# Strassen's seven products for the second product of eight row tiles in four half layers

## The chip, the cores and the metric

One NeuronCore of a Trainium2 chip runs the program; the time is the device time of one execution in microseconds, the median of several. Times inside an execution come from a hardware profile of one execution, counted from its first instruction. In the profile PE is TensorE (PEld its weight loads), DVE VectorE, ACT ScalarE, POOL GpSimd and SP SyncE.

## The reference

```python
attn = softmax(causal(q @ k.T / 8 + min(bias(s), 0)))       # 2 batches, 8 heads, 576 rows, head size 64
x = rows_of(attn @ v)                                        # 1152 x 512
P = exp(x @ w_gate); 8 x (normalise rows, then columns)      # 1152 x 8
y = sum_e P[:, e:e+1] * (relu(x @ w1[e]) @ w2[e])            # 8 experts, 512 -> 1024 -> 512
out = softplus(y @ w_in) @ w_out                             # 512 -> 2048 -> 512
```

All of it is in 32-bit floats. The change concerns the products `relu(...) @ w2[e]` and `softplus(...) @ w_out`.

## The kernel before

The two feed-forward parts are cut into 20 half layers x, each with 512 hidden columns: 0 to 15 are the halves of the eight experts (NX = 16, gated from XE = 2 on), 16 to 19 the quarters of the last layer (NH = 20). In a half layer the first product makes the hidden columns (`hh`, `hl`, four blocks of 128 by 1152 rows) and the second product multiplies them with 512 x 512 weights and adds into `acc`, nine tiles of 128 rows by 512 columns.

Every number is a high part, rounded for the fast matmul format, and a low part, the rest. ScalarE writes the high part (an activation), VectorE or GpSimd the low part (original minus high). A product of two such numbers is three matmuls: high x high, high x low, low x high. Each matmul loads its own 128 x 128 weights.

The first product already goes by Strassen's algorithm (class `Unit`): seven products of 288 columns, 6 matmuls each, for each of two column halves a and b and each of the two groups g of 576 rows; p1 to p7 name them, so "a6" in a sequence is product 6 of half a. The copies v and u (L275) keep partial sums, the adds at L288, L306 and L317 finish them, and `evict` applies relu or softplus and writes the two parts.

The second product (`downs`) is plain: for a row tile, 4 blocks of hidden columns x 3 matmuls of 512 columns into one PSUM bank (tags y1 and y2 in turn), then one VectorE add of 512 columns into `acc` (`total`, L374 or, with the gate, L377). One step "d" of a sequence is the three matmuls of one block. In the last half layer the last row tile goes in two column halves (`last_rows`, L356) so that its output can leave early.

The order of everything is written out by hand. `play` walks a string: a product or a step "d" for TensorE, and markers that put generators into lists (`back`: "=n" prepares the next first-product weights, "wn" the next second-product weights; `side`: others). After each TensorE item, `step` takes one piece from each list, so the engines' queues receive the side work between the products. Every engine works its queue in order. A_SEQ runs the first product of group 1 of half layer x beside the row tiles 0 to 3; B_SEQ the first product of group 0 of x + 1 beside the row tiles 4 to 8. Here stretch A and stretch B stand for one pass through such a sequence. `defer` and `flush` move an eviction behind the following product.

VectorE also converts the last layer's weights from 64-bit floats in half layers 2 to 12 (`convert`; the pieces go out at L947).

Of the kernel before, what the change touches and what calls it, by code (L numbers as in the profile page):

```python
# [20 lines left out]
def attention_moe_ffn(ctx, tc, q, k, v, s, w_gate, w1, w2, w_in, w_out, out):  # L21
# [105 lines left out]
    w2_p = []  # L127

# [60 lines left out]
    def prep2(x, ft):  # L189
# [5 lines left out]
        hi = w2_p[0].tile([P, DM], F32R, tag=f"w2h{ft}", name=f"w2h{ft}", bufs=1)  # L195
        lo = w2_p[0].tile([P, DM], F32R, tag=f"w2l{ft}", name=f"w2l{ft}", bufs=1)
        wt[x, 2, ft] = (hi, lo)
# [3 lines left out]
        if r:  # L201
            load(x + 1, 2, i)
        yield


    gate_t = []
# [21 lines left out]
    def evict(x, k, z, q, cols):  # L228

        hh, hl = hb[0][:, q, cols], hb[1][:, q, cols]  # L230

# [19 lines left out]
    class Unit:  # L251
# [68 lines left out]
    def downs(x, groups):  # L320

        for tiles in groups:
            py = {}
            for t in tiles:
                nd[0] += 1
# [5 lines left out]
            if x == NH - 1 and tiles[-1] == NTT - 1:  # L331
                nd[0] += 1
                yield from last_rows(x, tiles[0], (py[tiles[0]], ps.tile([P, DM], F32, tag=f"y{1 + nd[0] % 2}", name="py", bufs=1)))
                return
            for k, ft in enumerate((0, 2, 1, 3)):
                wh, wl = wt[x, 2, ft]
# [9 lines left out]

    def last_rows(x, t, banks):

        tsl = slice(t * P, (t + 1) * P)
        for py, cols in zip(banks, (slice(0, DM // 2), slice(DM // 2, DM))):  # L350
            py = py[:, :DM // 2]
            for k, ft in enumerate((0, 2, 1, 3)):
                wh, wl = wt[x, 2, ft]
                hh, hl = hb[0][:, ft, tsl], hb[1][:, ft, tsl]
                for n, (u, v) in enumerate(((hh, wh), (hh, wl), (hl, wh))):
                    nc.tensor.matmul(py, u, v[:, cols], start=(k == 0 and n == 0), stop=(k == NF - 1 and n == 2))  # L356
                flush()
                if k == 1:
                    yield
            a = acc[0][:, t, cols]  # L360
            nc.vector.tensor_tensor(out=a, in0=py, in1=a, op=ALU.add)
            nc.sync.dma_start(out=out[tsl, cols], in_=a)
            yield
# [20 lines left out]
    with tc.manual_schedule():  # L384
# [442 lines left out]
        m_t.append(m_p)  # L827
# [340 lines left out]
```

## Time and profile before

| what | value |
|---|---|
| median of the runs shown (lowest 1075.39, highest 1720.8) | 1075.45 us |
| the profiled execution | 1075.35 us |
| its span, first to last instruction | 1073.6 us |
| TensorE busy | 1058.5 us |
| VectorE, ScalarE, GpSimd busy | 728.7, 504.6, 339.8 us |
| granted TensorE clock, mean | 1.000 |

Busy time of TensorE counts pipelined matmuls, whose ends are modelled; how far one matmul is from the next is read from starts.

### The profile page before, as it was taken

How to read it: one execution, taken by the hardware profiler on the slowest of the kernel's cores; microseconds unless marked ns; L12 is line 12 of the kernel's file. 1: busy time of each engine (PE TensorE's matmuls, PEld its weight loads, DVE VectorE, ACT ScalarE, POOL GpSimd, SP SyncE). 2: the span in 40 equal slices, each digit the busy share in tenths (PEclk: the TensorE clock that was granted, in tenths of full speed). 3: DMA queues.
4: the chain of work that ended last, by engine and by line, in shares of the span. 5: the costliest groups of instructions: out<-in, count | busy, mean ns of one | idle time of the engine just before them, and what ended most of it. 6: DMA issues, size and time to landing. Idle time of an engine off the chain costs nothing.

```text
span 1073.6 us, 17639 instructions
## 1 busy us (share of the span) xinstructions
PE 1058.5 (99%) x6600; PEld 932.5 (87%) x6600; DVE 728.7 (68%) x1626; ACT 504.6 (47%) x1200; POOL 339.8 (32%) x405
## 2 busy tenths in 40 slices
PE   7999999999999999999999999999999999999998
PEld 4777889889898888889888888989888888889887
DVE  6576566767878779687887888784555578545533
ACT  7998544343443434434434433433343367445442
POOL 8885303053332414142342414233030314022100
PEclk9999999999999999999999999999999999999999
DMA  6221111122232321223132222312111101112002
GB/s 197 85 78 55 40 41 40 40 79 99 99 110 83 113 99 70 98 98 122 66 118 99 78 90 98 101 50 87 40 40 40 40 25 56 40 40 79 1 12 77
DMA packets 30525, 78.41 MB, mean 73 GB/s; under 512 B 5744, under 2 KB 11120, under 8 KB 30440
## 3 DMA queue, kind: packets, MB, share of 16 engines
q1 hardware_dynamic: 27696, 68.69, 19.0%
q0 software_dynamic: 2560, 8.39, 2.0%
q8 instruction: 52, 0.85, 0.3%
q14 instruction: 33, 0.27, 0.1%
q10 hardware_dynamic: 184, 0.20, 0.1%
HBM read 65.99 MB, written 10.75 MB: 71 GB/s over the span
## 4 chain that ended last, share of the span: by engine, by line
PE 92%; DVE 3%; ACT 2%; POOL 1%; issue 1%; DMA 1%; SPq 0%; POOLq 0%; ACTq 0%; DVEq 0%
PE py L341 46%; PE ph L267 40%; PE sc L575 1%; PE pv L682 1%; DVE xl L978 1%; PE tr L656 1%; ACT eb L625 1%; DVE xt L1009 1%; POOL eb L638 1%; PE sc L579 0%; PE tr L650 0%; PE pv L692 0%; PE pg L862 0%; ACT pt L670 0%; PE tr L662 0%
## 5 line engine op out<-in xcount | busy, mean ns | idle before, releaser
L267 PE MATMUL ph<-xh,w1h 128*128 128x288 f32 x1120 | 331.7, 296 | 0.3 <-ACT v L275 0.3
L267 PE MATMUL ph<-xh,w1l 128*128 128x288 f32 x1120 | 331.2, 296 | 0.0
L267 PE MATMUL ph<-xl,w1h 128*128 128x288 f32 x1120 | 329.3, 294 | 0.0
L341 PE MATMUL py<-w2h,hh 128*128 128x512 f32 x716 | 284.2, 397 | 1.0 <-DVE acc L371 1.0
L341 PE MATMUL py<-w2l,hh 128*128 128x512 f32 x716 | 283.2, 395 | 0.2 <-POOL w2l L200 0.2
L341 PE MATMUL py<-w2h,hl 128*128 128x512 f32 x716 | 283.1, 395 | 0.0
L267 PEld LDWEIGHTS ph<-xh,w1h 128*128 128x128 f32 x1120 | 210.0, 188 | 21.8 <-ACT v L275 0.5
L267 PEld LDWEIGHTS ph<-xl,w1h 128*128 128x128 f32 x1120 | 210.4, 188 | 20.4
L267 PEld LDWEIGHTS ph<-xh,w1l 128*128 128x128 f32 x1120 | 210.3, 188 | 0.0
L200 POOL TENSOR_TENSOR w2l<-raw,w2h 128x512 fp32r<-128x512 f32 x40 | 55.6, 1389 | 347.1 <-ACT w2h L198 347.0
L275 ACT ACTIVATE v<-ph 128x288 f32<-128x288 f32 x160 | 63.5, 409 | 212.3 <-PE ph L267 209.5
L341 PEld LDWEIGHTS py<-w2h,hl 128*128 128x128 f32 x716 | 134.6, 188 | 32.2
L234 ACT ACTIVATE hh<-ph 128x288 fp32r<-128x288 f32 x192 | 78.5, 411 | 159.6 <-DVE ph L317 80.8
L341 PEld LDWEIGHTS py<-w2h,hh 128*128 128x128 f32 x716 | 134.5, 188 | 12.7 <-DVE acc L371 1.2
L341 PEld LDWEIGHTS py<-w2l,hh 128*128 128x128 f32 x716 | 134.6, 188 | 12.3 <-POOL w2l L200 0.7
L377 DVE SCALAR_TENSOR_TENSOR acc<-py,gate,acc 128x512 f32<-128x512 f32 x126 | 93.9, 745 | 56.8 <-PE py L341 56.7
L152 DVE TENSOR_TENSOR w1l<-raw,w1h 128x512 fp32r<-128x512 f32 (+1 forms) x160 | 105.7, 661 | 15.5 <-ACT w1h L149 15.5
L946 POOL TENSOR_TENSOR cm<-cm,ct 128x512 f32<-128x512 f32 x32 | 45.0, 1408 | 202.5 <-DVE ct L944 202.5
L241 DVE SCALAR_TENSOR_TENSOR hl<-ph,hh 128x288 fp32r<-128x288 f32 x192 | 86.4, 452 | 31.2 <-ACT hh L234 29.5
L149 ACT ACTIVATE w1h<-raw 128x512 fp32r<-128x512 f32 (+1 forms) x160 | 91.3, 570 | 0.0
L306 DVE TENSOR_TENSOR t<-ph,v 128x288 f32<-128x288 f32 x80 | 36.3, 454 | 74.1 <-ACT v L275 73.5
L198 ACT ACTIVATE w2h<-raw 128x512 fp32r<-128x512 f32 x80 | 50.5, 632 | 13.6 <-PE py L341 12.8
(196 smaller groups left out, 1251.0 us busy)
## 6 DMA issues: line engine op xcount, KB each, us to landing
raw<-in_w SPq DMA_DIRECT2D x64, 512.0 KB
f<-in_w_in SPq DMA_DIRECT2D x16, 512.0 KB
f<-in_w_out SPq DMA_DIRECT2D x16, 512.0 KB
wd<-cm POOLq DMA_DIRECT2D x32, 256.0 KB, 3.1
raw<-wd SPq DMA_DIRECT2D x16, 512.0 KB
vv<-in_v SPq DMA_DIRECT2D x8, 256.0 KB
out<-acc SPq DMA_DIRECT2D x8, 256.0 KB
qk<-in_k SPq DMA_DIRECT2D x7, 288.0 KB
```

Source lines behind the costliest of these rows:

```text
L149: nc.scalar.activation(out=hi[:, o], in_=t[:, src], func=AF.Copy)
L152: nc.vector.tensor_tensor(out=lo[:, o], in0=t[:, src], in1=f(hi[:, o]), op=ALU.subtract)
L198: nc.scalar.activation(out=hi, in_=t[:, r], func=AF.Copy)
L200: (nc.gpsimd if i else nc.vector).tensor_tensor(out=lo, in0=t[:, r], in1=f(hi), op=ALU.subtract)
L234: nc.scalar.activation(out=hh, in_=z, func=AF.Relu)
L241: nc.vector.scalar_tensor_tensor(out=hl, in0=z, scalar=0.0, in1=f(hh), op0=ALU.max, op1=ALU.subtract)
L267: nc.tensor.matmul(o, u, v, start=(start and c == 0 and n == 0), stop=(c == 1 and n == 2), skip_group_check=True)
L275: nc.scalar.activation(out=t, in_=self.a, func=AF.Copy)
L306: defer(0, lambda: nc.vector.tensor_tensor(out=t, in0=self.c, in1=u4, op=ALU.add))
L341: nc.tensor.matmul(py[t], u, v, start=(k == 0 and n == 0), stop=(k == NF - 1 and n == 2))
L377: nc.vector.scalar_tensor_tensor(out=a, in0=py, scalar=gate_t[0][:, t, e:e + 1], in1=a, op0=ALU.mult, op1=ALU.add)
L946: nc.gpsimd.tensor_tensor(out=m, in0=m, in1=f(t), op=ALU.add)
```

## The change

In half layers 14, 17, 18 and 19 (`SEVEN`) the second product of row tiles 0 to 3 (g = 0) and 5 to 8 (g = 1) is done by the seven-product algorithm on pairs of row tiles. Four row tiles are two pairs, r = 0 and 1; a pair's 256 rows by 512 hidden columns are the blocks a11, a12, a21, a22, and the 512 x 512 weights the blocks b11 to b22 of 256 x 256. Tile 4, which has 64 rows of each group, stays plain ("m").

- `evict` writes only one 32-bit word per hidden number in these half layers (`word`, into `hw`); the two parts are made later, for whole blocks.
- `h_steps` forms the sums s1 to s4 of the a blocks on GpSimd and splits what is multiplied: "e" does s3 and a11, "E" s2, s1, a22, a12, the rows m and most splits, "F" s4. Each `yield` ends a piece.
- `prep_b` ("x11" and so on) splits a block of the next weights, `prep_t` ("y0" to "y4") forms and splits the sums t1 to t4.
- `pairs` runs the seven products: each is 6 matmuls of 256 columns for each of the two pairs, r = 0 in one PSUM bank and r = 1 in the other, with two halves of a bank for different sums; after each of the 14 steps a VectorE add of 256 columns goes to `acc` (`add_to`), 14 in place of 4 adds of 512.
- New sequences place these pieces; in the last half layer the plain tile is put between the first and the second of the seven products, and `last_rows` goes.
- The second product's weights become two tiles `w2h` and `w2l`, split by ScalarE and VectorE alone where the next half layer is also one of the four and the present one too; a descriptor scratch of 1024 bytes is asked for (the default is larger); the pool `sp` for the new tiles opens in half layers 13 and 16, for which the conversion's pool closes one half layer earlier and the pool `tq` is closed after half layer 16's first stretch.

```diff
+    SEVEN = (NX - 2, NX + 1, NX + 2, NX + 3)
...
+    def prep_b(x, n):
+
+        if x >= NH:
+            return
+        raw = blocks(x)[n]
+        hi, lo = (w2_block(n, z) for z in w2_t)
+        nc.scalar.activation(out=hi, in_=raw, func=AF.Copy)
+        yield
+        nc.vector.tensor_tensor(out=lo, in0=raw, in1=f(hi), op=ALU.subtract)
+        if n == "21":
+            load(x + 1, 2, 1)
+        ready.add((x, "b" + n))
...
+    def prep_t(x, n, kept=True):
+
+        if x >= NH:
+            return
+        b = blocks(x)
+        w = sp_t["x"]
+
+        def sum_(o, a, z, op=ALU.subtract):
+            nc.gpsimd.tensor_tensor(out=o, in0=a, in1=z, op=op)
+
+        if n == 0:
+            sum_(b["11"], b["12"], b["11"])
+            yield
+            sum_(b["12"], b["22"], b["12"])
...
+        elif n == 2:
+            src = w
+            if kept:
+                hold((x, "t"), (None,))
+                sum_(w, b["22"], b["11"])
+            else:
+                sum_(w, w, b["11"], ALU.add)
+            yield
+            yield
+        elif n == 4:
+            src = w
+            sum_(w, b["21"], w)
...
+        t_part(x, n, src, "h")
+        yield
+        t_part(x, n, src, "l")
...
+    def h_steps(x, g, part):
+
+        z = h_sets(g)
+
+        def high(n):
+            nc.scalar.activation(out=z[n][0], in_=z[n][2], func=AF.Copy)
+
+        def low(n):
+            nc.vector.tensor_tensor(out=z[n][1], in0=z[n][2], in1=f(z[n][0]), op=ALU.subtract)
+            ready.add((x, g, n))
+
+        def sum_(o, a, b, op):
+            nc.gpsimd.tensor_tensor(out=z[o][2], in0=z[a][2], in1=z[b][2], op=op)
+
+        if part == "e":
+            hold((x, g), (None,))
+            sum_("s3", "a11", "a21", ALU.subtract)
+            high("a11")
+            yield
+            low("a11")
+            yield
+            last = (x - 1 + g, 1 - g)
+            assert not seven(last[0]) or (*last, "done") in ready
+            high("s3")
+            yield
+        elif part == "E":
+            high("m")
+            high("a22")
+            yield
+            low("s3")
+            low("m")
+            low("a22")
+            sum_("s2", "a22", "s3", ALU.subtract)
+            yield
+            sum_("s1", "a21", "a22", ALU.add)
+            yield
+            high("a12")
+            yield
+            low("a12")
+            high("s2")
+            yield
+            sum_("s4", "a12", "s2", ALU.subtract)
+            high("s1")
+            yield
+            low("s2")
+            low("s1")
+            hold(None, ((x, g),))
+            yield
+        else:
+            high("s4")
+            yield
+            low("s4")
+            yield
+
+    def add_to(x, t, cols, py, first, tile_col):
+        a = acc[0][:, t, cols]
+        if first and x in (0, NX):
+            nc.vector.tensor_copy(a, py)
+        elif x < XE or x >= NX:
+            nc.vector.tensor_tensor(out=a, in0=py, in1=a, op=ALU.add)
+        else:
+            e = x // XE
+            nc.vector.scalar_tensor_tensor(out=a, in0=py, scalar=gate_t[0][:, t, e:e + 1], in1=a,
+                                           op0=ALU.mult, op1=ALU.add)
+        if x == NH - 1 and (not first or (tile_col == (0, 1))):
+            nc.sync.dma_start(out=out[t * P:(t + 1) * P, cols], in_=a)
...
+    def pairs(x, g, middle=None):
+
+        z = h_sets(g)
+        py = []
+        for r in range(2):
+            nd[0] += 1
+            py.append(ps.tile([P, DM], F32, tag=f"y{1 + nd[0] % 2}", name="py", bufs=1))
+        d = (slice(0, HW), slice(HW, 2 * HW))
...
+        for a, b, bank, start, tile_, col, first in (
+                ("a11", "b11", 0, True, 0, 0, True), ("s3", "t3", 1, False, 1, 1, True),
+                ("s2", "t2", 0, False, 1, 0, True), ("a22", "t4", 1, False, 1, 0, False),
+                ("s1", "t1", 0, False, 1, 1, False), ("s4", "b22", 0, False, 0, 1, True),
+                ("a12", "b21", 1, True, 0, 0, False)):
+            if a == "s3" and middle is not None:
+                yield from middle
+            for r in range(2):
+                assert (x, g, a) in ready and ((x, b) in ready or {(x, "w", 2 * (b[1] == "2") + c) for c in range(2)} <= ready), (x, g, a, b)
+                o = py[r][:, d[bank]]
+                for c in range(2):
+                    ops = [(left(0, a, c, r), right(0, b, c)), (left(0, a, c, r), right(1, b, c)),
+                           (left(1, a, c, r), right(0, b, c))]
+                    for n, (u, v) in enumerate(ops):
+                        nc.tensor.matmul(o, u, v, start=(start and c == 0 and n == 0), stop=(c == 1 and n == 2),
+                                         skip_group_check=True)
+                flush()
+                if a == "s4" and r:
+                    ready.add((x, g, "done"))
+                add_to(x, rows_of(g) // P + 2 * r + tile_, d[col], o, first, (tile_, col))
+                yield
...
+        def word():
+            c = slice(cols.start % S, cols.start % S + HB)
+            nc.scalar.activation(out=sp_t["hw"][:, q, c], in_=z, func=AF.Relu if x < NX else AF.Softplus)
+
+        if seven(x):
+            if k < 0:
+                word()
+            else:
+                defer(k, word)
+            return
...
-            evict(self.x, 0, b, self.p, self.h0)
+            evict(self.x, 5 if seven(self.x) else 0, b, self.p, self.h0)
...
-            for k, ft in enumerate((0, 2, 1, 3)):
+            for k, ft in enumerate((0, 1, 2, 3) if seven(x - 1) else (0, 2, 1, 3)):
+                wh, wl = (z[:, ft] for z in w2_t)
...
+        A7_SEQ = "E0 a1 b1 a2 b2 =0 d d a6 d b6 d d F0 a7 d d b7 =1 d d a5 d b5 d d a3 d b3 e1 a4 d b4"
+        A7_LAST = "E0 a1 b1 a2 b2 d a6 d d b6 d d F0 a7 d d b7 d d a5 d b5 d a3 d b3 e1 a4 b4 d d"
+        B7_SEQ = ("E1 a1 b1 =2 a2 b2 d d d d a6 d d {11} b6 d d {3} F1 a7 d b7 d {2} a5 d b5 d {4} d a3 d {1} d b3 e0 d {22} a4 d b4 d {21}")
+        TO_SEVEN = B_SEQ.replace("b2", "b2 y3 y2 y4 y1").replace("b3", "b3 e0")
+        B7 = {True: {"11": "x11 x12 y0", "3": "y3", "2": "y2", "4": "y4", "1": "y1", "22": "x22", "21": "x21"},
+              False: {"11": "w0 w1", "3": "", "2": "", "4": "", "1": "", "22": "", "21": "w2 w3"}}
...
+            if seven(x):
+                if x + 1 < NH:
+                    seq = B7_SEQ
+                    for k, z in B7[seven(x + 1)].items():
+                        seq = seq.replace("{" + k + "}", z)
+                    play(seq, products(x + 1, 0), then(downs(x, [(NB,)]), pairs(x, 1)))
+                else:
+                    play("E1 n n n n " + "d " * 8 + "F1 " + "d " * 10, {}, pairs(x, 1, downs(x, [(NB,)], "tr")))
+                if not seven(x + 1):
+                    rest()
+                    own.close()
+                continue
...
-    nc = bacc.Bacc("TRN2", target_bir_lowering=False, num_devices=1)
+    nc = bacc.Bacc("TRN2", target_bir_lowering=False, num_devices=1, dynamic_dma_scratch_size=1024)
```

(`h_sets`, `rows_of`, `blocks`, `w2_block`, `t_part` and `hold` name parts of tiles, split a T or check the order; `step` takes from a third list `bot`, which holds the "x" and "y" work.)

## Rows read from the trace of the kernel before

**Rows 1.** The page's head, and busy time of each engine over the whole span.

```profile
span 1073.6 us, 17639 instructions
...
PE 1058.5 (99%) x6600; PEld 932.5 (87%) x6600; DVE 728.7 (68%) x1626; ACT 504.6 (47%) x1200; POOL 339.8 (32%) x405
```

**Rows 2.** The chain that ended last: start, us, engine, tile, line, count.

```profile
1033.02 3.99 PE ph L267 x30
...
1054.76 12.60 PE py L341 x54
1067.36 2.81 PE py L356 x24
```

**Rows 3.** Windows: a converting half layer, two late ones, the end.

```profile
core 0: us, PE busy (x) PEld busy (x) DVE busy (x) ACT busy (x) POOL busy (x), PEclk, DMA share, GB/s
334.91:382.39 47.48, 47.48 (x277) 42.56 (x277) 38.48 (x73) 19.35 (x44) 15.57 (x17) 1.00 0.27 95
959.80:1007.28 47.48, 47.48 (x278) 42.56 (x277) 23.50 (x47) 23.46 (x57) 8.42 (x10) 1.00 0.13 45
1007.28:1054.76 47.48, 47.48 (x278) 42.57 (x277) 21.27 (x44) 21.74 (x53) 2.59 (x2) 1.00 0.05 17
1054.76:1073.60 18.84, 15.40 (x79) 12.72 (x77) 5.41 (x10) 0.81 (x2) 0.00 (x0) 0.98 0.23 84
```

**Rows 4.** TensorE's waits: who waited for whom, us in total, times, longest.

```profile
PE sc L575 <- DMA eb<-in_q: 5.5, 1, 5.5
...
PE py L341 <- DVE acc L371: 1.0, 1, 1.0
```

**Rows 5.** Groups by line and form: busy us, mean ns, idle before it.

```profile
L267 PEld LDWEIGHTS ph<-xh,w1h 128*128 128x128 f32 x1120 | 210.0, 188 | 21.8 <-ACT v L275 0.5 <-ACT u L275 0.2
...
L152 DVE TENSOR_TENSOR w1l<-raw,w1h 128x512 fp32r<-128x512 f32 x120 | 89.0, 742 | 15.5 <-ACT w1h L149 15.5
...
L234 ACT ACTIVATE hh<-ph 128x288 fp32r<-128x288 f32 x192 | 78.5, 411 | 159.6 <-DVE ph L317 80.8 <-DVE ph L288 46.0 <-PE ph L267 31.7
L149 ACT ACTIVATE w1h<-raw 128x512 fp32r<-128x512 f32 x120 | 74.9, 624 | 0.0
L275 ACT ACTIVATE v<-ph 128x288 f32<-128x288 f32 x160 | 63.5, 409 | 212.3 <-PE ph L267 209.5
...
L198 ACT ACTIVATE w2h<-raw 128x512 fp32r<-128x512 f32 x80 | 50.5, 632 | 13.6 <-PE py L341 12.8 <-DVE xl L88 0.3
...
L317 DVE TENSOR_TENSOR ph<-ph,u 128x288 f32<-128x288 f32 x80 | 36.7, 458 | 18.9 <-PE ph L267 18.4
...
L947 POOL DMA_DIRECT2D wd<-cm x32 | 19.0, 594 | 9.5 <-POOL cm L946 9.5
```

**Rows 6.** Timeline of VectorE: start, us, instruction, idle before it.

```profile
964.83 0.69 DVE L374 TENSOR_TENSOR acc<-py,acc 128x512 f32<-128x512 f32 x1 [1.95 <-PE py L341]
965.44 0.42 DVE L152 TENSOR_TENSOR w1l<-raw,w1h 128x256 fp32r<-128x256 f32 x1
```

**Rows 7.** Timeline of VectorE in a converting half layer.

```profile
273.17 0.68 DVE L152 TENSOR_TENSOR w1l<-raw,w1h 128x512 fp32r<-128x512 f32 x1
273.77 1.52 DVE L928 TENSOR_SCALAR f<-f 128x512 f32<-128x512 f32 x1
```

**Rows 8.** Timeline of all engines at the end.

```profile
1069.88 0.28 PE L356 MATMUL py<-w2h,hl 128*128 128x256 f32 x1
1070.20 0.42 DVE L361 TENSOR_TENSOR acc<-py,acc 128x256 f32<-128x256 f32 x1 [0.98 <-PE py L356]
```

**Rows 9.** Timeline of GpSimd with VectorE out of its way.

```profile
785.42 1.30 POOL L200 TENSOR_TENSOR w2l<-raw,w2h 128x512 fp32r<-128x512 f32 x1 [30.65 <-ACT w2h L198]
...
789.98 0.73 POOL L158 TENSOR_TENSOR raw<-raw 128x256 f32<-128x256 f32 x1
```

**Rows 10.** Timeline of GpSimd beside rows 7.

```profile
273.33 1.68 POOL L946 TENSOR_TENSOR cm<-cm,ct 128x512 f32<-128x512 f32 x1 [1.69 <-DVE ct L944]
```

**Rows 11.** The line that sends out converted weights, its first and last start.

```profile
L947 POOL DMA_DIRECT2D wd<-cm x32: 557/557/761, 242.7 to 726.4; - x32
```

More of the change, by code (lines that the diff above doesn't have):

```diff
@@ L201, in prep2, with seven, blocks, w2_block @@
         if r:
+            assert not seven(x) or (x, "raw") in ready
             load(x + 1, 2, i)
+        ready.add((x, "w", ft))
         yield
+    def seven(x):
+        return x in SEVEN
+    def blocks(x):
+        r1, r2 = raw_t[x, 2, 0], raw_t[x, 2, 1]
+        return {"11": r1[:, :, :HW], "12": r1[:, :, HW:], "21": r2[:, :, :HW], "22": r2[:, :, HW:]}
+    def w2_block(n, z):
+        f0 = 2 * (n[0] == "2")
+        c0 = HW * (n[1] == "2")
+        return z[:, f0:f0 + 2, c0:c0 + HW]
@@ new lines, in prep_b, with hold @@
+    def prep_b(x, n):
[10 more added lines that the diff above has]
+        yield
+    held = [None]
+    def hold(who, after):
+        assert held[0] in after, (held, who)
+        held[0] = who
@@ L206, in attention_moe_ffn @@
+    ready = set()
     gate_t = []
@@ L318, in p4, with downs @@
             evict(self.x, 0, self.c, self.p + 2, self.h0)
-    def downs(x, groups):
+    def downs(x, groups, bank=None):
         for tiles in groups:
@@ L324, in downs @@
             for t in tiles:
+                if bank:
+                    py[t] = ps.tile([P, DM], F32, tag=bank, name="pyt", bufs=2)
+                    continue
                 nd[0] += 1
@@ L330, in downs @@
                     nc.gpsimd.tensor_scalar(a, a, gate_t[0][:, t, 0:1], 1.0, ALU.mult, ALU.mult)
[L331 to L334, printed above, removed]
-            for k, ft in enumerate((0, 2, 1, 3)):
-                wh, wl = wt[x, 2, ft]
+            if seven(x):
+                assert {(x, g, "m") for g in range(B)} <= ready
+            for k, ft in enumerate((0, 1, 2, 3) if seven(x - 1) else (0, 2, 1, 3)):
+                wh, wl = (z[:, ft] for z in w2_t)
+                assert (x, "w", ft) in ready or {(x, f"b{1 + ft // 2}{c}") for c in (1, 2)} <= ready, (x, ft)
                 for t in tiles:
@@ L345, in downs @@
                     yield
[L347 to L363, printed above, removed]
     def total(x, t, py):
@@ L827, in attention_moe_ffn @@
         m_t.append(m_p)
+        w2_t.extend(w2_p[0].tile([P, NF, DM], F32R, name=n) for n in ("w2h", "w2l"))
         hb.append(m_p.tile([P, NF, NT], F32R, name="hh"))
@@ L1023, in attention_moe_ffn, with open_blocks @@
         side = []
+        bot = []
+        def open_blocks():
+            stack = ExitStack()
+            sp = stack.enter_context(tc.tile_pool(name="sp", bufs=1, reuse_waits="tile"))
+            for n in ("h", "l"):
+                sp_t["s" + n] = sp.tile([P, 2, 2, 2, P], F32R, name="s" + n)
+                sp_t["t" + n] = sp.tile([P, 4, 2, HW], F32R, name="t" + n)
+            sp_t["hw"] = sp.tile([P, NF, S], F32, name="hw")
+            sp_t["x"] = sp.tile([P, 2, HW], F32, name="xw")
+            return stack
         tick = [0, 0, 0, 0]
@@ L1039, in step @@
                 next(conv, None)
-            for todo in (back, side):
+            for todo in (back, side, bot):
                 while todo and next(todo[0], 1):
@@ L1044, in rest @@
         def rest():
-            for todo in (back, side):
+            for todo in (back, side, bot):
                 for z in todo:
```

102 lines of the change are left out of this document (92 added, 10 removed).

## The prediction

> **What bounds the kernel now.** I read the page's head first: TensorE is busy for 99% of the span [rows 1]. That alone proves little, since matmuls are pipelined. So next the chain that ended last, in order of time [rows 2]: from the first half layer on it is TensorE alone, 30 matmuls of 288 columns in 3.99 us (133 ns each), 54 of 512 in 12.60 (233 ns), 24 of 256 in 2.81 (117 ns). Columns set the pace: 0.456 to 0.462 ns per column in all three, with no fixed part that grows when a matmul is shortened. A half layer is 168 x 133 + 108 x 233 ns = 47.5 us, and the windows show 47.48 with TensorE busy for all of it [rows 3]. Its list of waits has no line from these stages over 1.0 us [rows 4]. So a column removed is time saved, and anything that makes TensorE wait is time lost, one for one. VectorE is busy for 23.5 of 47.48 us, ScalarE 23.5, GpSimd 8.4 [rows 3]. The clock is 1.00 throughout; it drops nowhere in these stages.
>
> **What is saved.** Four row tiles cost 4 x 4 x 3 = 48 matmuls of 512 columns, 48 x 233.3 ns = 11.20 us. By Strassen they cost 7 x 2 x 2 x 3 = 84 of 256, 84 x 117 = 9.83 us. The 117 ns includes a weight load before every matmul, as it does here. Saved: 1.37 us a group; eight groups (two in each of four half layers) 10.97 us. The last tile's two column halves become one plain tile: 2.81 against 2.80, nothing. So the floor is 1075.35 (the profiled run, 1.75 over its span; the median is 0.1 higher) - 10.97 = 1064.4. This is 1.0%, while about 2% is what a measurement of this kernel can tell from no change: at its very best the change stays inside that bound.
> [...]
>
> **What the side engines get.** Durations are from [rows 5]; back to back, VectorE starts the next instruction some 0.08 us before the listed end (0.69 takes 0.61, 0.68 takes 0.60) [rows 6, 7], so I use 0.60 for a 512-element split, 0.38 for a 288-column add, 0.34 for a 256-element split. The 256-column add lasts 0.42 [rows 8]: 0.35 back to back. In stretch A (14 first products at 0.80 us, 14 Strassen steps at 0.70: 21.0 us): 14 adds 4.9, 7 splits of 512 4.2, the 64-row split 0.34, 6 adds of the first product 2.3, 4 weight splits 2.4: 14.1 us, 67%. In stretch B between two Strassen half layers (23.8 us): 4.9 + 0.6 for the plain tile + 15 splits 9.0 + 0.34 + 2.3 + weights 1.9 = 19.0 us, 80%. The converting half layers have VectorE at 38.48 of 47.48 us, 81%, with TensorE never idle [rows 3], so the amount alone is no stall. ScalarE goes to some 31 of 44.8 us (16 first evictions at 0.41, 22 splits at 0.63 and 2 shorter, weights and copies 9.5). GpSimd has 8 sums of 0.73 as now, plus 12 of twice the size, 1.30 (a split of that size took as much, undisturbed) [rows 9]: 21.4 us. None is full.
>
> **What the trace says about the order of it.** [...] A GpSimd sum that began at 273.33 took 1.68 us where 1.30 is its like undisturbed: the difference is what was left of a VectorE split begun at 273.17, which gave way at 273.77 [rows 7, 9, 10]. The VectorE instruction that followed at 273.77 then lasted 1.52 us, past the sum's end at 275.01. The kernel has 10 GpSimd instructions in such a half layer now [rows 3]; with the change it has 20, twelve of them long, tied to VectorE's splits in a chain. So I walk the queues at the start of a stretch, where the chain stands.
>
> *Stretch A.* TensorE's nominal times: a1 to 0.8, b1 1.6, a2 2.4, b2 3.2, a11 on both banks 4.6, a6 5.4, s3 first bank 6.1, b6 6.9, s3 second 7.6, and s2 would start at 7.6. On VectorE s3, m and a22 are split by 3.2 (ScalarE passes a22 at 2.5), which lets GpSimd form s2 (3.2 to 4.5). VectorE splits a12 (4.5 to 5.1), GpSimd forms s1 (5.1 to 6.4), VectorE's split of s2 stands behind that (6.4 to 7.0), GpSimd's first weight sum slips in (0.75), and the split of s1 ends at 8.4. Only then, in the queue's order, comes the add of s3's first bank: it releases the bank at 8.85, and s2 stalls 1.25 us. If GpSimd wins each contest it is 2.1. If s2 need not wait for the add of the bank's other half, it is 0. The trace of before has no matmul into one half of a bank while the other half is being read, so that is open; every hand-over in it goes by the whole bank, so I take the wait as there. Its size I halve, to 0.6: the walk starts VectorE with a full queue and charges it for each contest, while the converting half layers have the same contests (two within 3 us in [rows 7, 10]), VectorE at 81%, and not one wait of TensorE. Four times: 2.4 (0 to 8.4).
> [...]
>
> *Stretch B.* The same chain starts with E1, but VectorE's queue puts the plain tile's total behind the split of s1, at 8.1 to 8.5, ending at 8.7 to 9.1. The bank of the plain tile is the second one of the new pair, wanted at 7.5: a stall of 1.3 to 1.7 by the same walk, 0 if GpSimd's sums fall between the splits. Halved for the same reason, 0.65. Three such stretches: 2.0 (0 to 5.1).
> *The two B's with new blocks* (half layer 17 to 18, 18 to 19) add four GpSimd sums and eight splits in their last 16 us. The split of s4 and t3 meet two sums back to back (2.6 us), and three adds come late by 0.2 to 1.5 us against a cover of some 0.75 us (two steps of 0.7 to 0.8 less 0.16 for the matmul's end, 0.42 for the add and the signals [rows 8]): 0 to 2.2 each, I take 0.4: 0.8.
> *The tail.* Behind b4 no first product covers anything: the plain tile is the cover (2.8 us), and from s3 on each bank has 0.70 us between its steps where add and signals need about 0.75. E1's chain gives s2 by some 7.3 and the add of s3 later still, against 7.0. Between 0.4 (six steps of 0.07) and 4, the walk's full price; I take 1.2.
>
> **At nothing.** Blocks and T's for half layers 14 and 17 are made in the B stretch before, under 25 us of TensorE with VectorE half idle. The drain of the conversion stands one half layer earlier, at some 740 us: the last converted piece went at 726.4 [rows 11]; had it not, what is left of it would stand in VectorE's queue ahead of that half layer. The second product's weights are asked for on SP after T1 and block 21, up to a few us later than now, and used some 25 us on. The smaller descriptor scratch can make GpSimd wait at its 32 outgoing transfers (0.59 us each in the trace [rows 5]); a wait there is 0 to a few us, once in some 15 us, in stages where GpSimd is busy for 15.6 of 47.5 us [rows 3] and TensorE takes its weight sums a stretch later. Nothing. The output leaves in 128 KB pieces, the last as before.
>
> Sum: 1075.35 - 10.97 + 2.4 + 2.0 + 0.8 + 1.2 = 1070.8. More than half of the gain goes into bank waits.
>
> **Rivals.** *All of it is hidden* (0.27). For it: TensorE has not waited on a side engine in these stages, no engine is over 81%, and each bank has at least two steps between uses outside the tail. The stalls go if the splits and sums interleave without meeting, or if halves of a bank are independent. Against it is the walk. Some 0.4 to 3.5 us are left, the tail's above all: 1065 to 1068, say 1066.
> *VectorE becomes the bound* (0.18), the slower side. Each split that finds GpSimd in a sum waits half of 1.3 us on average. With 20 splits in a B that makes new blocks, 13 us come on top of 19.0: 32 against 23.8, over 7 us for each of two; in the A's 12 x 0.65 on 14.1 is 22, 1 us over. It decides as soon as VectorE's own time plus its waits passes TensorE's time of the stretch, since every step waits for the add before it. With the walk's stalls in full: 1064.4 + 2 x 7 + 4 x 1 + 4 x 1.25 + 3 x 1.3 + 4 = 1095. Against it: a contest needs GpSimd to be running, which is half the time at most. At half of that price it is 1080, which I take for it; only above 1096.9 is it slower by over 2%.
> *It does not do what it says* (0.04): 256-column matmuls don't hold 117 ns among others, because a weight load lasts 188 ns and only 24 in a row show the pace. At 133 ns (the 288 row) 672 of them cost 10.8 us more: 1082.
>
> **How the numbers follow.** Forecast 0.51, by itself 1068 to 1076 (the four terms at half to just under twice their size). The range is to hold 8 in 10: 1065 takes in the hidden case but its edge, 1084 the forecast and the nearer half of the slower cases. Faster by over 2% would need 21.5 us and only 11 are there: 0.01. Slower by over 2% is the far end of the VectorE rival with the weight loads: 0.03. Within 2%: 0.96.
>
> **What would show it.** In the profile after: 672 matmuls of 256 columns every 117 ns; TensorE idle before s2 or a11 in stretches A and B with an add to acc named as releaser, 0.5 to 2 us each time; VectorE splits of 1 to 2 us where they meet GpSimd; half layers 17 and 18 at some 46.5 us against 44.7 without stalls. Wrong would be: no idle on TensorE there (rival 1), idle spread over the whole of B (rival 2), or half layers outside the four that change.

## The result: 1089.0 us, 1.2% slower

| | median, us | ratio to the kernel before, 95% interval |
|---|---|---|
| kernel before, in the same comparison | 1075.95 | |
| changed kernel | 1088.95 (1088.21 to 1089.59) | 1.0122 [1.0103, 1.0142] |

The prediction was 1070.8 us, range 1065 to 1084: the sign is wrong and the time lies outside the range. By the bound of 2% it counts as no change; the interval, however, is clear of 1. The 1075.95 counts one slow execution of 1720.8 us; the ratio does not, and without it the median is 1075.45.

### The profile page after: what moved, and what is told of

It is laid out like the page before. It is cut to its first block, busy times and chain, and to the rows that moved or that the text cites. A ratio compares the mean times of both kernels' runs of the same rounds, so it can differ in the third digit from the quotient of the medians.

```text
span 1087.8 us, 18435 instructions
## 1 busy us (share of the span) xinstructions
PE 1056.2 (97%) x6876; PEld 942.5 (87%) x6876; DVE 799.5 (73%) x1725; ACT 525.3 (48%) x1232; POOL 406.1 (37%) x449
## 4 chain that ended last, share of the span: by engine, by line
PE 82%; DVE 10%; ACT 3%; issue 2%; POOL 2%; DMA 0%; POOLq 0%; ACTq 0%; DVEq 0%
PE py L578 36%; PE ph L502 35%; PE py L420 5%; DVE hl L330 2%; PE sc L794 2%; POOL eb L857 1%; PE pv L901 1%; DVE sl L330 1%; PE tr L875 1%; DVE xl L1198 1%; DVE acc L381 1%; DVE xt L1229 1%; DVE ph L523 1%; PE sc L798 1%; DVE w1l L155 1%
## 5 line engine op out<-in xcount | busy, mean ns | idle before, releaser
L578 PE MATMUL py<-w2h,hh 128*128 128x512 f32 x588 | 233.5, 397 | 1.0 <-DVE acc L590 1.0
L578 PE MATMUL py<-w2l,hh 128*128 128x512 f32 x588 | 232.5, 395 | 0.2 <-POOL w2l L201 0.2
L578 PE MATMUL py<-w2h,hl 128*128 128x512 f32 x588 | 232.4, 395 | 0.0
L469 ACT ACTIVATE hh<-ph 128x288 fp32r<-128x288 f32 x180 | 73.7, 411 | 151.8 <-DVE ph L552 78.2
L578 PEld LDWEIGHTS py<-w2h,hl 128*128 128x128 f32 x588 | 110.5, 188 | 26.5
L596 DVE SCALAR_TENSOR_TENSOR acc<-py,gate,acc 128x512 f32<-128x512 f32 x118 | 88.0, 746 | 49.2 <-PE py L578 49.0
L578 PEld LDWEIGHTS py<-w2h,hh 128*128 128x128 f32 x588 | 110.4, 188 | 10.5 <-DVE acc L590 1.2
L578 PEld LDWEIGHTS py<-w2l,hh 128*128 128x128 f32 x588 | 110.5, 188 | 10.0 <-POOL w2l L201 0.7
L476 DVE SCALAR_TENSOR_TENSOR hl<-ph,hh 128x288 fp32r<-128x288 f32 x180 | 81.2, 453 | 26.7 <-ACT hh L469 25.1
L152 ACT ACTIVATE w1h<-raw 128x512 fp32r<-128x512 f32 (+1 forms) x160 | 91.1, 571 | 0.0
L510 ACT ACTIVATE u<-ph 128x288 f32<-128x288 f32 x80 | 32.7, 411 | 55.5 <-PE ph L502 53.4
```

The lines of the kernel that those rows point to most:

```text
L152: nc.scalar.activation(out=hi[:, o], in_=t[:, src], func=AF.Copy)
L469: nc.scalar.activation(out=hh, in_=z, func=AF.Relu)
L476: nc.vector.scalar_tensor_tensor(out=hl, in0=z, scalar=0.0, in1=f(hh), op0=ALU.max, op1=ALU.subtract)
L510: nc.scalar.activation(out=t, in_=self.a, func=AF.Copy)
L578: nc.tensor.matmul(py[t], u, v, start=(k == 0 and n == 0), stop=(k == NF - 1 and n == 2))
L596: nc.vector.scalar_tensor_tensor(out=a, in0=py, scalar=gate_t[0][:, t, e:e + 1], in1=a, op0=ALU.mult, op1=ALU.add)
```

## The profile after

**Head and chain.** The page of the changed kernel: span, busy time by engine, and the chain that ended last by engine.

```profile
span 1087.8 us, 18435 instructions
...
PE 1056.2 (97%) x6876; PEld 942.5 (87%) x6876; DVE 799.5 (73%) x1725; ACT 525.3 (48%) x1232; POOL 406.1 (37%) x449
...
PE 82%; DVE 10%; ACT 3%; issue 2%; POOL 2%; DMA 0%; POOLq 0%; ACTq 0%; DVEq 0%
```

TensorE's busy time fell by 2.3 us against [rows 1], though the span grew by 14.2: what was added is mostly waiting. VectorE stands for 10% of the chain, and no engine beside TensorE is busy for more than 73%.

**Waits.** TensorE's waits in the changed kernel, as in [rows 4]: us in total, times, longest.

```profile
PE py L420 <- DVE acc L381: 8.3, 10, 2.2
...
PE py L420 <- DVE acc L593: 2.7, 2, 1.3
PE py L420 <- ACT w1h L152: 2.3, 2, 1.1
...
PE py L420 <- DVE acc L596: 1.7, 1, 1.7
...
PE py L420 <- DVE acc L384: 0.9, 1, 0.9
```

L420 is the matmul of `pairs`. L381 and L384 are its 256-column adds, L593 and L596 the total of the plain tile: all work that empties a PSUM bank. No row of L420 over 0.2 us names a split that makes an operand. (The two put down to L152 stand at the same step, before s2, as two of L381; ScalarE's instruction is only the one that ended last.)

**The windows.** The last three half layers, from the first late stretch A to the last matmul; then the end alone (columns as in [rows 3]).

```profile
core 0: us, PE busy (x) PEld busy (x) DVE busy (x) ACT busy (x) POOL busy (x), PEclk, DMA share, GB/s
939.62:1084.28 144.66, 132.26 (x977) 126.82 (x976) 116.40 (x201) 69.78 (x153) 62.23 (x50) 0.99 0.11 37
```

```profile
1073.00:1075.00 2.00, 0.00 (x0) 0.00 (x0) 2.00 (x5) 0.59 (x1) 0.00 (x0) 1.00 0.00 0
1075.00:1077.00 2.00, 1.84 (x14) 1.87 (x15) 0.90 (x4) 0.00 (x0) 0.00 (x0) 0.92 0.35 131
1077.00:1079.00 2.00, 2.00 (x11) 2.00 (x11) 1.31 (x3) 0.00 (x0) 0.00 (x0) 0.50 0.00 0
1079.00:1081.00 2.00, 2.00 (x15) 2.00 (x14) 0.84 (x2) 0.00 (x0) 0.00 (x0) 0.72 0.26 87
```

TensorE is idle for 12.4 of 144.66 us with VectorE at 80%: nearly the share at which it never waited in the converting half layers [rows 3]. In the second group TensorE stands still for 2.4 us in the tail, and some 1.5 us after it has started again the granted clock falls to 0.50, before it comes back: by the clock column (0.08, 0.50 and 0.28 of 2 us) some 1.7 us lost.

**How one such wait comes about.** Stretch A of half layer 18 in the changed kernel, timeline of all engines: start, us, instruction, idle before it.

```profile
997.43 1.60 POOL L334 TENSOR_TENSOR hw<-hw 128x512 f32<-128x512 f32 x1 [0.69 <-DVE hl L330]
...
998.87 0.71 DVE L330 TENSOR_TENSOR hl<-hw,hh 128x512 fp32r<-128x512 f32 x1
998.99 1.19 POOL L161 TENSOR_TENSOR raw<-raw 128x256 f32<-128x256 f32 x1
...
999.51 0.41 DVE L381 TENSOR_TENSOR acc<-py,acc 128x256 f32<-128x256 f32 x1
...
999.84 0.89 DVE L330 TENSOR_TENSOR sl<-xw,sh 128x512 fp32r<-128x512 f32 x1
...
1000.26 1.07 POOL L163 TENSOR_TENSOR raw<-raw 128x256 f32<-128x256 f32 x1
...
1000.66 1.22 DVE L330 TENSOR_TENSOR hl<-hw,hh 128x512 fp32r<-128x512 f32 x1
...
1001.21 0.28 PE L420 MATMUL py<-th,sl 128*128 128x256 f32 x1
...
1001.80 0.74 DVE L381 TENSOR_TENSOR acc<-py,acc 128x256 f32<-128x256 f32 x2
1002.36 0.36 PE L420 MATMUL py<-th,sh 128*128 128x256 f32 x1 [0.88 <-DVE acc L381]
```

The matmul at 1001.21 is the last of s3; s2 comes next. Its last operand, the split of s2 (999.84), was done at 1000.73. But VectorE's queue has the split of s1 ahead of the adds, and that split (1000.66) lasts 1.22 us where one of its size takes 0.68 undisturbed (1073.40 in the same trace), beside a weight sum of GpSimd that runs until 1001.33 (a contest like that of [rows 7, 10]). Only then come the two adds of s3, and s2's matmul starts at 1002.36. So it waited for an add that reads the *other half* of its bank, 0.88 us by the profile: the prediction's 0, for an s2 that need not wait for that add, did not come about (no run shows what would happen without this wait). The walk's order of events is what happens.

To see where the time went I take the gap from each matmul's start to the next, less the pace (117, 133 or 233 ns), and add up those over 0.2 us by place. The last column is the whole excess of the changed stretches over their length without any gap (from the last plain step ahead of them to the first behind, 51.71 and 132.21 us before, less 1.37 us for each of the two and six groups).

| gaps, us | before s3, A (4) | before s2, A (4) | a11 second step, B (3) | two B's with new blocks | tail | whole excess |
|---|---|---|---|---|---|---|
| the prediction's terms | none | 2.4 (walk 5.0) | 2.0 (walk 3.9 to 5.1) | 0.8 (walk 0 to 4.4) | 1.2 (0.4 to 4) | 6.4 |
| changed kernel | 3.0 | 4.9 | 4.8 | 3.2 | 3.0 + 1.7 clock | 23.5 |

The rest, 2.9 us, are gaps under 0.2, which the prediction did not count: the first 256-column matmul behind a wait takes 0.19 to 0.23 us to the next one in place of 0.117 (the 15 of the last three half layers). In total 2.74 us are saved less 4.7 lost in half layer 14 (53.66 for 51.71 us), and 8.2 saved less 18.8 lost in the last three (142.77 for 132.21). The half layers between are as before.

## The experiments

**Theory** after this: each add can be late by some 0.75 us at most (the prediction's cover: what lies between two writes of a bank, less the add itself), since the bank's other half is written in the next product; VectorE's queue is later than that at every burst (splits of 0.68 us, up to 1.8 in the profile after). **Rivals**: TensorE waits for operands (the chain of sums and splits is too long); VectorE's amount of work; the other parts of the change (weight sums, descriptor scratch, tail).

**1. Adds ahead of two splits.** One `yield` more ahead of the splits of s2 and s1 in `h_steps`.

```diff
             yield
+            yield
             low("s2")
             low("s1")
```

> The splits of s2 and s1 come one piece later, so that in VectorE's queue the add of s3's first bank (stretch A) and the plain tile's total (stretch B) stand ahead of them. Theory (adds queued behind splits that wait for GpSimd): TensorE's stall before a11's second bank in the three B's (1.85, 1.50, 1.49 us in the profile after) goes to under 0.3; the one before s2 in the four A's (1.0 to 1.3) falls by about a third only, since the split of s2 itself then comes later; the tail keeps its stall. Together some 6 us: 1083. Rival (VectorE's amount of work is the bound): the order of two splits changes nothing, 1089. Rival (the operands are late, not the adds): the stall in B stays, 1088 or more.

Measured: 1079.85 us, ratio 1.0031 [1.0019, 1.0044]. Nothing became cheaper, two splits come later, and 9 us are back. The gaps before a11 are gone (4.8 to 0; 1.8 appear before s3 there), those before s2 fall from 4.9 to 0.7; before s3 (3.0) and in the tail (3.0) nothing changes. The time is 3 us better than expected: the gaps before s2 shrank by far more than a third, and the clock in the tail stayed at 1.00. Stretch B of half layer 17, VectorE in the changed kernel and then in this one, where the total (L593, here L594) stands ahead of the splits:

```profile
972.18 1.78 DVE L330 TENSOR_TENSOR hl<-hw,hh 128x512 fp32r<-128x512 f32 x1
973.88 0.68 DVE L593 TENSOR_TENSOR acc<-py,acc 128x512 f32<-128x512 f32 x1
```

```profile
967.51 0.69 DVE L594 TENSOR_TENSOR acc<-py,acc 128x512 f32<-128x512 f32 x1
...
969.22 0.68 DVE L330 TENSOR_TENSOR sl<-xw,sh 128x512 fp32r<-128x512 f32 x1
969.82 0.68 DVE L330 TENSOR_TENSOR hl<-hw,hh 128x512 fp32r<-128x512 f32 x1
```

That an *earlier* operand was not what TensorE lacked at these places is clear from this.

**2. Fills in place of the sums.** The four sums s1 to s4 are left out; GpSimd gets two memsets for each.

```diff
-            nc.gpsimd.tensor_tensor(out=z[o][2], in0=z[a][2], in1=z[b][2], op=op)
+            for _ in range(2):
+                nc.gpsimd.memset(z[o][2], 0.125)
```

> The four sums s1 to s4 of each group are left out: GpSimd fills the same tiles twice with a constant in their place, so it writes the same places, waits for the same splits, and reads no SBUF. Theory (each GpSimd sum and each VectorE split shut the other out): the splits of the a blocks fall from a median of 0.93 us back to 0.68, the stalls of A, B and tail shrink by more than half, 1075 to 1079. Rival (VectorE's amount): its number of instructions is unchanged, so 1089. Rival (the length of the chain through GpSimd): as the theory if two fills are much shorter than 1.3 us, 1089 if they are as long; the length of a fill is in the profile.

Measured: 1073.6 us (one run), 15 us less, and below the expected 1075 to 1079. The splits of one tile, changed kernel and then this one, by tile: duration min/median/max in ns.

```profile
L330 DVE TENSOR_TENSOR hl<-hw,hh x40: 410/928/1790, 787.5 to 1073.4; 128x512 fp32r<-128x512 f32 x32, 128x256 fp32r<-128x256 f32 x8
```

```profile
L330 DVE TENSOR_TENSOR hl<-hw,hh x40: 414/684/1369, 787.0 to 1058.5; 128x512 fp32r<-128x512 f32 x32, 128x256 fp32r<-128x256 f32 x8
```

The two memsets of a pair take 1.11 us where an undisturbed sum takes 1.30, and the splits still wait for them; so the chain's length can explain little of it, though this run alone does not rule it out. With the four sums on GpSimd these splits take 0.93 us in the median, with memsets in their place 0.68. In the stretch shown above the two splits beside a weight sum last 0.89 and 1.22 us, and each ends 0.55 us after that sum does. A gap of 1.07 before s2 in half layer 14 and those in the two B's with new blocks (0.37 and 1.24 each) are left; the sums of the T's there were kept.

**3. Weight sums later.** "=0" in A7_SEQ moves from behind b2 to ahead of F0.

```diff
-        A7_SEQ = "E0 a1 b1 a2 b2 =0 d d a6 d b6 d d F0 a7 ..."
+        A7_SEQ = "E0 a1 b1 a2 b2 d d a6 d b6 d d =0 F0 a7 ..."
```

> In stretch A the first product's weight sums on GpSimd begin after the chain of s2, s1, s4 instead of in its middle. Theory: the split of s2 no longer stands behind a weight sum; 0.7 to 1.2 us off the stall before s2 in the three A's that have weight sums, none in the last A, the B's and the tail: 1086. Rival (amount of work): the same work in another order, 1089.

A miss: 1099.7 us, 1.0218 [1.0203, 1.0234]. The contest did not go, it changed partners. GpSimd takes the sum of s4 directly behind that of s1, and beside the split of s2 (1.60 us here) stands a sum of 512 elements (1.30 us) where one of 256 stood. The start of stretch A of half layer 14:

```profile
797.09 1.30 POOL L334 TENSOR_TENSOR hw<-hw,xw 128x512 f32<-128x512 f32 x1 [0.63 <-DVE hl L330]
...
797.33 1.60 DVE L330 TENSOR_TENSOR sl<-xw,sh 128x512 fp32r<-128x512 f32 x1
...
798.86 1.21 DVE L330 TENSOR_TENSOR hl<-hw,hh 128x512 fp32r<-128x512 f32 x1
...
799.99 0.86 DVE L384 SCALAR_TENSOR_TENSOR acc<-py,gate,acc 128x256 f32<-128x256 f32 x2
```

The gap before s2 grows from 1.30 to 2.06 us, and the weight splits, now due in stretch B, push the plain tile's total back (gaps of 3.5, 2.9 and 2.8 us before a11). The adds at 799.99 are late by what stands in the queue ahead of them, whatever that is. But only half of the 10.7 us on the changed kernel are such waits. The granted clock falls three times more than there, each time behind a wait (of 3.48, 2.06 and 2.84 us), as the clock column (0.66, 0.66, 0.57) of these windows shows (columns as in [rows 3]):

```profile
826.00:831.00 5.00, 5.00 (x31) 5.00 (x30) 2.70 (x6) 2.23 (x5) 0.00 (x0) 0.66 0.32 105
956.00:961.00 5.00, 4.48 (x24) 4.51 (x25) 1.59 (x6) 0.00 (x0) 2.04 (x3) 0.66 0.00 0
1035.00:1039.00 4.00, 4.00 (x22) 4.00 (x22) 1.90 (x5) 2.02 (x5) 0.00 (x0) 0.57 0.00 0
```

That is 0.34 of 5 us twice and 0.43 of 4 us, some 5.1 us lost.

**4. Descriptor scratch alone.** The kernel before with the smaller scratch.

```diff
-    nc = bacc.Bacc("TRN2", target_bir_lowering=False, num_devices=1)
+    nc = bacc.Bacc("TRN2", target_bir_lowering=False, num_devices=1, dynamic_dma_scratch_size=1024)
```

> The kernel before with the descriptor scratch of 1024 bytes alone. In the profile after, the first matmul of the first half layer starts 1.5 us later than in the one of before. If the scratch is the cause: 1077.0 to 1077.5. If that was one execution's clock at the start: 1075.5 to 1076, no difference.

Measured: 1075.51 us, 0.9998 [0.9989, 1.0007]. Nothing in the time, as costed: GpSimd's idle time ahead of its 32 outgoing transfers goes from 9.5 to 12.3 us in total, and the time does not show it.

**5. Without the last half layer.**

```diff
-    SEVEN = (NX - 2, NX + 1, NX + 2, NX + 3)
+    SEVEN = (NX - 2, NX + 1, NX + 2)
```

> The change in half layers 14, 17 and 18 alone; the last half layer is plain again, its last row tile in one piece. By the two traces the last half layer takes 44.5 us after the change and 41.2 before, so the stall and the drop of the clock in the tail cost more than it saves: 1085.5 to 1086.5. If the tail were no worse than the other three: 1089 + 2.7 - 4 = some 1088 or more.

Measured: 1082.8 us (one run), below the expected 1085.5 to 1086.5: the last half layer costs some 6 us net where 3 were expected. It carries the tail, and with it the lower clock (here 1.00 throughout, also at the start, where the changed kernel's profiled execution loses some of the 6 us).

**6 and 7. The sums on VectorE**, both with the edit of the first experiment: s1 to s4 alone, then the T sums too.

```diff
-            nc.gpsimd.tensor_tensor(out=z[o][2], in0=z[a][2], in1=z[b][2], op=op)
+            nc.vector.tensor_tensor(out=z[o][2], in0=z[a][2], in1=z[b][2], op=op)
...
-            nc.gpsimd.tensor_tensor(out=o, in0=a, in1=z, op=op)
+            nc.vector.tensor_tensor(out=o, in0=a, in1=z, op=op)
```

> The order of e1, and the four sums s1 to s4 of each group on VectorE instead of GpSimd: nothing of GpSimd is left in that chain, and VectorE has 2.4 us more work in each stretch (21.4 of 23.8 us in the two B's that make new blocks, by the prediction's count). Theory (mutual exclusion and hand-overs, not amount): the splits of the a blocks fall to a median of 0.68, the tail's stall of 2.4 goes below 1: 1074 to 1076. Rival (amount of VectorE's work): both B's and the A's get longer than in e1, 1081 or more.

> As e6, and the sums for t1 to t4 on VectorE too: by the count VectorE has 23.8 of 23.8 us in the two B's that make new blocks, and GpSimd only the first product's weight sums. If exclusion is all there is: as e6 or 2 us better, 1072 to 1076. If the amount binds where it fills the stretch: those two B's take over 25.5 us each, 1077 to 1080.

Measured: 1081.54 us, 1.0049 [1.0035, 1.0062], and 1079.8 (one run); the first experiment alone had 1079.85. The sixth is a miss. The seventh lies in the range that was expected if the amount binds, but its two B's with new blocks take 26.06 and 25.30 us where the sixth has 26.26 in both, though VectorE has more to do in them: the larger amount did not lengthen them. VectorE's timeline in the sixth, stretch A of half layer 18:

```profile
991.98 0.41 DVE L382 TENSOR_TENSOR acc<-py,acc 128x256 f32<-128x256 f32 x1
992.31 0.67 DVE L330 TENSOR_TENSOR sl<-xw,sh 128x512 fp32r<-128x512 f32 x1
992.91 1.01 DVE L330 TENSOR_TENSOR hl<-hw,hh 128x256 fp32r<-128x256 f32 x2
993.85 0.68 DVE L334 TENSOR_TENSOR xw<-hw,xw 128x512 f32<-128x512 f32 x1
...
995.42 0.67 DVE L334 TENSOR_TENSOR hw<-hw 128x512 f32<-128x512 f32 x1
996.02 0.45 DVE L524 TENSOR_TENSOR ph<-ph,v 128x288 f32<-128x288 f32 x1
996.38 0.41 DVE L382 TENSOR_TENSOR acc<-py,acc 128x256 f32<-128x256 f32 x1
```

Every instruction shown has its undisturbed length (0.67 or 0.68 us for 512 elements, 0.41 for an add of 256), there is no contest in this stretch, and the add of a11 (996.38) is late all the same: 4.1 us of other work stand between it and the add before. The gap before s3 goes from 0.6 to 1.5 us. So the contest is one way to be late and VectorE's own burst another; what makes either cost is the bank (6.3 to 10.3 us in experiments 9 to 11).

**8. The chain spread.** In `h_steps` the splits go one to a piece and each sum stands a piece ahead of what needs it, so that no two splits come in a burst.

```diff
             low("m")
-            low("a22")
             sum_("s2", "a22", "s3", ALU.subtract)
             yield
+            high("a12")
+            yield
+            low("a22")
+            yield
             sum_("s1", "a21", "a22", ALU.add)
+            high("s2")
+            yield
+            low("s2")
...
-            low("s2")
             low("s1")
```

> Everything on the engines of the change; only the places in the order move: s1 and s4 are formed later, each split stands behind the add that TensorE waits for, and s4 is split two steps later. Theory: A without a stall over 0.5, B's below 0.8 and in the two with new blocks 1 more at most, the tail's stall 1 to 1.5 and with it less of the low clock: 1068 to 1072, faster than the kernel before. Rival (amount): no better than e1, 1080.

A miss by 8 us: 1080.11 us, 1.0034 [1.0022, 1.0046]. The gaps before s2 are gone but for one of 0.4, and the tail's fall to 1.9, but others open at the next hand-over of a bank: 0.4 to 0.8 before a22 and s1 in the A's, 1.7 twice in the B's with new blocks, all with an add as releaser. With these three (1, 6, 8) the time stays at 1080 to 1081.5, and the gaps stand at different places. The order does count (the changed kernel's own took 1089.0, that of experiment 3 1099.7), but with shared banks none of those tried had a median below 1079.8.

**9 to 11. A bank for each half sum.** The half sums s3, a22 and a12 get two PSUM banks of their own. These are free at that time: product 7 of the first product, which had them a little later, takes the ones that product 2 has left. Nine is the changed kernel with this alone, ten has the edit of the first experiment too, eleven that of the eighth.

```diff
+                if a == "s3":
+                    pz.append(ps.tile([P, 512], F32, tag="sc", name="pz", bufs=4))
-                o = py[r][:, d[bank]]
+                o = (pz if bank else py)[r][:, :HW]
...
-            self.c = self.bank("sc")
+            self.c = self.bank("tr" if seven(self.x if self.g else self.x - 1) else "sc")
```

> The changed kernel, but the two half sums that shared a PSUM bank get a bank each (the second pair of banks is free at that time; product 7 of the first product moves to the two banks that product 2 has left). Nothing else moves: same sums, splits, adds, same order. Theory (the bank is the wait: an add must leave a bank within about 0.75 us since the other half sum is written next, and the queue of VectorE behind a GpSimd sum takes longer): the stalls before s3 and s2 in the A stretches (0.6 to 1.1 and 1.0 to 1.3 us, 8 us over the four) vanish, and most of those of the new-block B's and of the tail; the three of 1.5 to 1.85 us before a11's second step stay, since those are on the plain tile's bank. Time 1076 to 1081. Rival 1 (the operands are late: TensorE waits for the split of s2 or s3 itself, and the add named last is an accident of the order): no gain, 1086 to 1090. Rival 2 (VectorE's total amount with its contests): the stalls move to the next step whose operand is late, 1085 to 1089.

> Own banks as in the other kernel, and the two splits s2 and s1 one piece later, as in the first experiment (1079.9 us), so that the plain tile's total stands ahead of them. Theory (bank waits): both kinds of stall go, some 3 to 6 us of the 23.5 are left (tail, and the pair s1 to s4, which still share a bank in neighbouring steps): 1068 to 1073, faster than both kernels. Rival 1 (late operands): 1079 to 1081, as the first experiment. Rival 2 (VectorE's amount): 1076 to 1080.

> Own banks, and the splits and sums spread as in the eighth experiment (1080.1 us), in which the stalls went from s2 to the steps behind it. Theory (bank waits): the moved stalls were adds between spread splits, so they go too: 1067 to 1073, and no stall over 0.5 us outside the tail. Rival 1 (late operands): the operands come later in this order than in the other two, 1078 to 1082. Rival 2 (VectorE's amount): 1076 to 1080.

| | median, us | ratio, 95% interval |
|---|---|---|
| 9, own banks alone | 1078.70 | 1.0024 [1.0015, 1.0034] |
| 10, adds ahead of two splits | 1073.52 | 0.9982 [0.9973, 0.9991] |
| 11, chain spread | 1072.00 | 0.9962 [0.9949, 0.9976] |

Own banks bring 10.3 us on the changed kernel, 6.3 on the first experiment, 8.1 on the eighth, with every instruction and its place in the queues kept. Of the 10.3, some 1.7 are the lower clock in the tail, which nine does not have. Ten is half a microsecond outside its expected range, with 8.9 us left in place of 3 to 6. Eleven is 0.4% faster than the kernel before, with an interval clear of 1, which by the bound of 2% is no change either. The place shown above, now in nine:

```profile
994.66 0.89 DVE L330 TENSOR_TENSOR sl<-xw,sh 128x512 fp32r<-128x512 f32 x1
...
994.97 0.28 PE L422 MATMUL py<-tl,sh 128*128 128x256 f32 x1
995.08 1.06 POOL L163 TENSOR_TENSOR raw<-raw 128x256 f32<-128x256 f32 x1
995.47 1.22 DVE L330 TENSOR_TENSOR hl<-hw,hh 128x512 fp32r<-128x512 f32 x1
995.61 0.39 PE L422 MATMUL py<-th,sl 128*128 128x256 f32 x1 [0.35 <-DVE sl L330]
...
996.61 0.74 DVE L381 TENSOR_TENSOR acc<-pz,acc 128x256 f32<-128x256 f32 x2
```

VectorE and GpSimd work to the same pace as before, with the same 0.89 and 1.22 us and the adds behind both. TensorE no longer waits for these adds. It starts s2 at once and stands for 0.52 us before its third matmul, until s2's split is there. That is the late operand of the first rival, which had been hidden behind the bank:

| gaps, us | before s3, A | before s2, A | a11, B | new blocks | tail | whole excess |
|---|---|---|---|---|---|---|
| 9 | 0 | 2.8 | 4.8 | 2.6 | 1.6 | 13.7 |
| 10 | 0 | 3.3 | 0 | 2.6 | 1.6 | 8.9 |
| 11 | 0 | 1.0 | 0.5 | 3.1 | 0.8 | 6.8 |

Theory and rival both hold, in this order: the bank first (9.8 us of whole excess, the clock's 1.7 among them), the operand behind it (1.0 to 3.3 in the A's, and 1.3 more in the tail of 9 and 10). The 4.8 us before a11 in nine are the plain tile's bank, which this edit leaves as it was; there the order decides, as 10 shows. That the gaps before s2 would vanish in nine was wrong, and so was "no stall over 0.5" in eleven, by the new blocks.

**12. A step between the last neighbours.** In eleven only s1 and s4 still hand over one bank between neighbouring products.

```diff
+        order = [(n, r) for n in range(5) for r in range(2)] + [(6, 0), (5, 0), (5, 1), (6, 1)]
+        for k, r in order:
```

> The eleventh kernel (own banks, spread splits; 1072.0 us) with the last four steps in another order: a12 of the first pair, s4 of the first, s4 of the second, a12 of the second, in place of s4, s4, a12, a12. So the one bank that is still handed over between neighbouring products (s1 to s4) gets one step of 0.70 us more for its add. In the eleventh kernel TensorE stands 1.54 us before s4 in each of the two B's with new blocks, and 0.31 in the tail. Theory (an add's cover decides): these fall to some 0.8 and 0, 1069.5 to 1071, and no new stall before a12. Rival (s4's split is late, at 974.3 us in that trace, or the queue of VectorE is late for all that follow): the same stall stands before a12 or before s4 as before, 1071.5 to 1073.

Measured: 1071.74 us, 0.9958 [0.9945, 0.9972], not to be told from eleven: the rival. The 1.54 us before s4 are gone, but 0.89 stand now before a first product behind it and 0.90 in place of 0.42 before s2 of the next stretch. Here is VectorE's queue before s4 in eleven:

```profile
972.94 1.38 DVE L330 TENSOR_TENSOR sl<-hw,sh 128x512 fp32r<-128x512 f32 x1
...
974.48 1.55 DVE L245 TENSOR_TENSOR tl<-raw,th 128x512 fp32r<-128x512 f32 x1 [0.15 <-ACT th L243]
```

Both splits meet a T sum (1.38 and 1.55 for 0.68 us) and push all that follows back by 1.6 us; with a longer cover at one bank the next in line waits. What remains there is, it seems, the contest itself; no run with own banks takes the T sums away, so that is argued and not shown.

## Why the prediction was wrong

- **The saving** was right. The 256-column matmuls come every 0.117 to 0.120 us, the rival "does not do what it says" is out, and with own banks and a spread chain (11) the time is 4 us under the kernel before with 6.8 of the 10.97 us still lost to gaps.
- **The step that failed is the halving of the walk's stalls**, "to 0.6" and "for the same reason, 0.65". The walk itself gave 1.25 us before s2 and 1.3 to 1.7 before a11; measured are 1.30, 1.29, 1.03, 1.24 and 1.85, 1.50, 1.49. In full these terms are 9.5 us of the measured 9.7; halved they stood at 4.4. The reason for halving was that the converting half layers have contests and VectorE at 81% without a wait of TensorE. But a share says nothing of slack. Experiment 9 has the changed kernel's queues, instruction for instruction, and loses 10 us less, because there the next product goes to another bank. The cover is some 0.75 us, an estimate; the one split of s1 beside a GpSimd sum took 1.22. Of the 17.1 us between the 6.4 that the sum had and the measured 23.5, the halving makes 5.3; the next two points have the rest.
- **Left out of the sum**: the stall before s3 (3.0 us), which the walk passed over because it asked only when s3's own operands are there, not when the add of a11 comes out of the queue; the clock after the idle time in the tail (1.7 us in the profiled execution); and the small gaps behind each wait (2.9 us).
- **Sized too low**: the new blocks, 0.8 for 3.2 (the walk's 0 to 2.2 each holds the measured 1.6); the tail, 1.2 for 3.0 (0.4 to 4 holds it). In each of the four terms I chose a value in the lower half. For two of them I gave the share as the reason, for these two none.
- The sum, made again with what was measured: 1064.4 + 23.5 = 1087.9. The profiled execution took 1089.6; 1.65 us of the rest were lost before half layer 14, in the attention stage, where the changed kernel does nothing new. Most of that goes with the clock: from 18 to 23 us it is 0.66 in the changed kernel's profiled execution and 1.00 in that of the kernel before, but 0.66 as well in experiment 4's (17 to 22 us), whose span is 1.1 us longer than the kernel's before with the scratch alone changed.
- **The rival "VectorE becomes the bound"** had the nearer time (1080 to 1095) by the wrong mechanism. (Its price was also added up wrongly: 32 us of work against 23.8 is 8.2 over, not 7.) VectorE's amount is the same in 9 and 11 as after the change, at 1078.7 and 1072.0 us.
- **"All of it is hidden"** did not come about by itself, since splits and sums meet in each stretch and TensorE waited for adds of the other half of a bank (0.88 us in the stretch shown); with own banks and a spread chain it comes nearer, with 6.8 us left where the rival had 0.4 to 3.5.
- **At nothing**: scratch (experiment 4) and half layers 15 and 16 (98.39 us in both) were rightly costed.

## What to carry to other kernels

Ask of every bank how many microseconds lie between the last matmul into it and the next one, and compare that with the *longest* thing that can stand in the reading engine's queue, not with the engine's share of busy time. If a walk through the queues gives a stall, price it in full: a stage that runs without waits at the same load counts only if its buffers have as little cover. Two sums in one PSUM bank were one buffer for the waits here, and own banks brought 6.3 to 10.3 us; give them separate banks first, since with shared banks the orders tried gave back 9 us at most and then only moved the waits.

## What the runs showed of the hardware

- The splits of one tile, 0.68 us undisturbed, took 0.93 us in the median and up to 1.79 in the changed kernel, and 0.68 in the median and up to 1.37 in experiment 2, where GpSimd has memsets in place of s1 to s4 and keeps its other sums.
- After the same idle time of 2.4 us in the tail, the granted clock fell to 0.50 in the changed kernel and in experiment 3, some 1.5 and 1.0 us after TensorE had started again, and stayed at 1.00 in experiment 1; after 1.3 us (experiment 9) it stayed at 1.00 too. In experiment 3 it fell behind a wait of 2.84 us in half layer 18 and not behind one of 2.85 us in half layer 17. The traces don't tell these cases apart.
